# First four blocks' tokens loaded as whole rows and transposed by TensorE; weights decoded with shifts and an integer addition

## The chip, the cores and the metric

One core of a Trainium2 chip runs the kernel. Its engines are TensorE (PE; its weight loads are listed as PEld), VectorE (DVE), ScalarE (ACT), GpSimd (POOL) and SyncE (SP), which here only issues DMAs. Each engine works through its own queue in order. The metric is the time of one execution on the device in microseconds.

## The reference

Three stages, all in float32 on 4 x 4096 = 16384 tokens of 192 channels:

```python
w = softmax(weight)                        # 8 heads x 7 taps
x = causal_convolution(x, w)               # each head's 24 channels with that head's 7 taps,
                                           # zeros before each of the 4 sequences
h = x @ w_in;  x = (h * cos(h)) @ w_out            # 192 -> 2048 -> 192
h = x @ w_in2; out = elu(h) @ w_out2               # elu(h) = h if h > 0 else exp(min(h, 0)) - 1
```

The weights of the MLPs come to the kernel as float64, the tokens and the taps as float32.

## The kernel before

**Tiling.** The tokens are cut into 32 segments of 512 consecutive ones, and a block is 16 tokens of each segment: 512 columns, 32 blocks. Channels lie on partitions. An operand "a" has channels 0:128 of one block, an operand "c" channels 128:192 of two blocks, one above the other. To transpose, 32 channels of all segments are loaded onto 32 partitions (`load`, L219), with the six tokens ahead of the block (the halo), in rows of 32 floats; DVE's 32 x 32 transpose (L265) then makes segments into columns. Block 0's halo for segment 0 doesn't exist, so its loads leave partition 0 of 32 out (L228) and a further load fetches that segment (`load_first`, L230). The convolution is seven multiply-adds of shifted columns on DVE (L289, L291). For three operands of the start, two taps are taken by ScalarE and GpSimd instead (L283, L285, L294).

**Products.** A float32 product is made of float32r products: each operand is split into a rounded part h and a rest l. A step is one tile of 128 hidden units for one block: five matmuls into u (`emit_A`), the nonlinearity with ScalarE, DVE and GpSimd (L353, L364, L370, L378 for the first MLP), a split (L386 on ScalarE, L391 on GpSimd) and five matmuls into acc (`emit_B`), five steps later. 16 steps make a block's MLP. The first MLP runs on four blocks, then the second on the same four, and so on: 1024 steps, 10240 matmuls. The first two blocks' steps alternate at the start.

**Weights.** `prepare` (L461) brings all weights in pieces, in the order of their use. A piece is loaded as pairs of 32-bit words and decoded from float64 to float32 (`decode`, L136): two DVE instructions take the exponent and the upper significand out (L148, L149), two of ScalarE scale (L151, L152), two of DVE put in the sign and join (L154, L155), one of GpSimd multiplies (L157). Then ScalarE rounds it and GpSimd subtracts. `w_in` has pieces of 256 elements a partition (four of 128), 26 in all; `w_out` has 32 pieces of 192. Each step calls `next(prep)` twice, which advances every piece in flight (at most FLIGHT = 4) by one stage; `limit` bounds the pieces loaded or in flight, 6 for the first MLP and 2 for the second. `need` advances until a step's weights are there. The raw words of the first MLP's pieces lie in the slots in which the first MLP's results will stand later (`early_tile`), 12 slots of 512 floats.

**Order.** The first 74 steps and all before them are traced and ordered by Tile, which places each instruction in its engine's queue by a simulated time; from step 74 on the order is that of the program (`manual_schedule`). The convolution advances one instruction a step (`next(cq)`), pauses between steps 48 and 80, and is pushed when a block's split is due, seven steps before its first product.

Of the kernel before, what the change touches and what calls it, by code (L numbers as in the profile page):

```python
# [30 lines left out]
CONV_ON = 80  # L31
AUX = 2          # taps of a convolution that ScalarE and GpSimd take ...
AUXB = (("a", 0), ("c", 0), ("a", 1))  # ... in these, while the weights are prepared
# [3 lines left out]
def conv_then_two_mlps(ctx, tc, x, weight, w_in1, w_out1, w_in2, w_out2, out):  # L37
    """Softmax-weighted causal convolution, then two token-wise MLPs.

    Token t = i * J + j is column (j, i) of a transposed operand: 32 x 32  # L40
    transposes turn segments i into columns when the channels of a partition
    group of 32 are loaded onto it.  Matrix products are float32 products in
    three float32r passes: each operand is split exactly into a rounded part h
    and the rest l, and h*h + h*l + l*h are accumulated (l*l too where its rows
    are free).
    """
# [6 lines left out]
    J = T // Q           # tokens in a segment  # L53
    JB = N // Q          # and of them in a block
# [29 lines left out]
    wch = const.tile([P, 2, K], F32, name="wch")  # L84

    def channel_masks():
# [18 lines left out]
        # Each partition's channel takes its head's weights: 0:128, then 128:192 twice.  # L105
# [25 lines left out]
    def raw_tile(m, n):  # L131
        if m == 1:
            return early_tile(I32)[:, 0:2 * n].rearrange("p (n two) -> p n two", two=2)
        return None

    def decode(raw, load, shape):  # L136
# [3 lines left out]
        if raw is None:  # L140
            raw = stage.tile([P] + shape + [2], I32, tag="raw", name="raw", bufs=PRE2)
# [3 lines left out]
        ew = stage.tile([P, 2] + shape, F32, tag="ew", name="ew")  # L145
        ef, w = ew[:, 0], ew[:, 1]
        e, lof = ef.bitcast(I32), lo.bitcast(F32)
# [10 lines left out]
        yield w, ew  # L158

    def prep_w_in(m, half, f0, f1):  # L160
        src = (w_in1 if m == 1 else w_in2).bitcast(I32).rearrange("k (f two) -> k f two", two=2)
        a, b = f0 * P, f1 * P
        if half == 0:
# [3 lines left out]
            raw = raw_tile(m, b - a)  # L167
            for r in decode(raw, load, [b - a]):
                yield
            w, _ = r  # L170
# [4 lines left out]
        else:  # L175
            # The first half of the columns on partitions 0:64, the second on 64:128.
# [7 lines left out]
            raw = raw_tile(m, c - a)  # L184
            for r in decode(raw, load, [c - a]):
                yield
            w, ew = r
            h = ew[:, 0].bitcast(F32R)
            nc.scalar.activation(out=h, in_=w, func=AF.Copy)
            yield  # L190
            nc.gpsimd.tensor_tensor(out=w, in0=w, in1=f32(h), op=ALU.subtract)
            dst = f32(wi[m, "s"])
            for p, cs in parts:
                nc.sync.dma_start(out=dst[0:D2, :, cs], in_=ew[p])
                nc.sync.dma_start(out=dst[D2:P, :, cs], in_=ew[p] if m == 1 else ew[p, 0:1].to_broadcast([D2, 2, c - a]))
            yield

    def prep_w_out(m, f0, f1):
        src = (w_out1 if m == 1 else w_out2).bitcast(I32)[f0 * P:f1 * P, :]
        fs = slice(f0, f1)  # L200

        def load(raw):
            nc.sync.dma_start(out=raw, in_=src.rearrange("(k p) (d two) -> p k d two", p=P, two=2))

        for r in decode(None, load, [f1 - f0, D]):
            yield
        w, _ = r
        hi, mid = wo[m, "h"][:, fs, :], wo[m, "s"][:, fs, 0:D2]
        nc.scalar.activation(out=hi, in_=w[:, :, 0:P], func=AF.Copy)
        nc.scalar.activation(out=mid, in_=w[:, :, P:D], func=AF.Copy)  # L210
        yield
        nc.gpsimd.tensor_tensor(out=wo[m, "l"][:, fs, :], in0=w[:, :, 0:P], in1=f32(hi), op=ALU.subtract)
        nc.gpsimd.tensor_tensor(out=wo[m, "s"][:, fs, D2:P], in0=w[:, :, P:D], in1=f32(mid), op=ALU.subtract)
        yield

# [1 line left out]
    x_in, ys, xs = {}, {}, {}  # L217

    def load(t, p, b, ch):  # L219
        """Block b and the HALO before it, channels ch to ch + 32: on partitions  # L220
        p to p + 32 a segment each."""
        if b:
            j0 = b * JB
            nc.sync.dma_start(out=t[p:p + Q], in_=xseg[:, j0 - HALO:j0 + JB, ch:ch + Q])
        else:
# [384 lines left out]
```

## Time and profile before

| | |
|---|---|
| median of 3 runs | 2473.9 us (2472.33 to 2475.47) |
| profiled execution, first to last instruction (span) | 2471.2 us |
| PE busy | 2354.1 us, 95% |
| DVE busy | 1607.6 us, 65% |
| ACT busy | 1905.1 us, 77% |
| POOL busy | 1434.3 us, 58% |
| granted TensorE clock, mean | 0.994 |

The page gives no time for the profiled execution other than its span. Busy times of an engine are the union of its instructions; a mean duration in a group of instructions counts also the part in which an instruction overlaps the one ahead. Matmuls are pipelined, so 0.39 us of one matmul and 0.23 us from one to the next go together. "SPq" is SP's queue; an entry's time there is the time that the issue took.

### The profile page before, as it was taken

To read this page: it belongs to the slowest core of one execution; us is meant where nothing else is said; L and a number is where in the kernel's file an instruction comes from. 1 tells how busy PE (TensorE), PEld (TensorE's weight loads), DVE (VectorE), ACT (ScalarE), POOL (GpSimd) and SP (SyncE) were. 2 spreads that over 40 slices of the span, in tenths; PEclk is the share of its full clock that TensorE was granted. 3 is DMA by queue.
4 is the path that set the end of the run, shared out by engine and by line. 5 is a ranking of instruction groups with operands and counts; after the bars stand their busy time and mean duration, and the time that the engine had idled before them with its cause. 6 is when DMAs were issued, how large, how long until landed. Compare 5 with 4: busy or idle time off the path is not lost.

```text
span 2471.2 us, 32370 instructions
## 1 busy us (share of the span) xinstructions
PE 2354.1 (95%) x10240; PEld 1926.0 (78%) x10240; DVE 1607.6 (65%) x2373; ACT 1905.1 (77%) x3446; POOL 1434.3 (58%) x1186
## 2 busy tenths in 40 slices
PE   0678999999999999999999999999999999999999
PEld 0455688888888888888888888888888888888887
DVE  3999744994369933797349953599337973387433
ACT  2667878878787787877788787877878777878876
POOL 2777755555555555555555555555555555555555
PEclk9899999999999999999999999999999999999999
DMA  2422111110011100110011100111001100010000
GB/s 66 104 73 75 50 17 19 32 31 5 14 28 27 25 11 11 30 35 16 7 23 28 29 12 13 22 31 28 11 7 34 30 20 8 18 22 14 9 14 14
DMA packets 263733, 65.57 MB, mean 27 GB/s; under 512 B 243336, under 2 KB 252552, under 8 KB 263560
## 3 DMA queue, kind: packets, MB, share of 16 engines
q1 hardware_dynamic: 263560, 63.50, 12.7%
q8 instruction: 80, 1.31, 0.2%
q14 instruction: 93, 0.76, 0.1%
HBM read 29.91 MB, written 12.58 MB: 17 GB/s over the span
## 4 chain that ended last, share of the span: by engine, by line
PE 89%; DVE 7%; SPq 2%; issue 1%; DMA 1%; POOL 0%; ACT 0%; DVEq 0%; POOLq 0%; ACTq 0%
PE u L345 44%; PE acc L405 9%; PE acc L406 9%; PE acc L403 9%; PE acc L404 9%; PE acc L402 9%; DVE w L378 1%; SPq L228 1%; DVE w L364 1%; DVE ew L149 1%; DVE ew L148 1%; DVE ew L154 1%; DVE ew L155 1%; DVE y L291 1%; DMA raw<-in_moe_w_out_dram 0%
## 5 line engine op out<-in xcount | busy, mean ns | idle before, releaser
L391 POOL TENSOR_TENSOR gl<-w,gh 128x512 fp32r<-128x512 f32 x1024 | 1335.9, 1305 | 950.3 <-PE acc L406 630.6
L380 DVE SCALAR_TENSOR_TENSOR w<-w,u 128x512 f32<-128x512 f32 x512 | 352.2, 688 | 696.7 <-ACT w L372 674.4
L386 ACT ACTIVATE gh<-w 128x512 fp32r<-128x512 f32 x1024 | 643.6, 629 | 27.2 <-DVE w L378 13.6
L370 ACT ACTIVATE w<-w 128x512 f32<-128x512 f32 x512 | 323.5, 632 | 216.6 <-DVE w L364 212.5
L355 ACT ACTIVATE w<-u 128x512 f32<-128x512 f32 x512 | 305.6, 597 | 214.3 <-PE u L345 211.3
L405 PE MATMUL acc<-gl,wo_h 128*128 128x512 f32 x1024 | 401.8, 392 | 5.1 <-POOL gl L391 4.9
L378 DVE TENSOR_TENSOR w<-u,w 128x512 f32<-128x512 f32 x512 | 348.6, 681 | 85.3 <-ACT w L370 81.1
L402 PE MATMUL acc<-gh,wo_l 128*128 128x512 f32 x1024 | 400.8, 391 | 0.7 <-ACT gh L386 0.4
L403 PE MATMUL acc<-gh,wo_h 128*128 128x512 f32 x1024 | 400.0, 391 | 0.0
L406 PE MATMUL acc<-gl,wo_s 128*128 128x512 f32 x1024 | 399.9, 391 | 0.0
L404 PE MATMUL acc<-gh,wo_s 128*128 128x512 f32 x1024 | 399.8, 390 | 0.0
L364 DVE SCALAR_TENSOR_TENSOR w<-u,w 128x512 f32<-128x512 f32 x512 | 347.1, 678 | 6.1 <-ACT w L353 5.9
L345 PE MATMUL u<-x,wi_s 128*128 128x512 f32 x1024 | 319.8, 394 | 7.3 <-DMA x<-cl 7.3
L372 ACT ACTIVATE w<-w 128x512 f32<-128x512 f32 x512 | 316.5, 618 | 0.1
L345 PE MATMUL u<-z,wi_s 128*128 128x512 f32 x1024 | 315.7, 390 | 0.0
L353 ACT ACTIVATE w<-u 128x512 int32<-128x512 f32 x512 | 298.6, 583 | 18.3 <-PE u L345 15.5
L291 DVE SCALAR_TENSOR_TENSOR y<-xT,wch,y 128x512 f32<-128x512 f32 x282 | 296.7, 1052 | 0.2
L345 PE MATMUL u<-xh,wi_l 128*128 128x512 f32 x512 | 205.9, 402 | 95.4 <-ACT xh L317 51.8
L405 PEld LDWEIGHTS acc<-gl,wo_h 128*128 128x128 f32 x1024 | 192.8, 188 | 52.2 <-POOL gl L391 12.9
L345 PEld LDWEIGHTS u<-x,wi_s 128*128 128x128 f32 x1024 | 194.4, 190 | 49.1 <-DMA x<-cl 8.0
L402 PEld LDWEIGHTS acc<-gh,wo_l 128*128 128x128 f32 x1024 | 193.0, 189 | 43.0 <-ACT gh L386 2.5
L404 PEld LDWEIGHTS acc<-gh,wo_s 128*128 128x128 f32 x1024 | 193.0, 188 | 40.6
(73 smaller groups left out, 2831.7 us busy)
## 6 DMA issues: line engine op xcount, KB each, us to landing
out_dram<-o SPq DMA_DIRECT2D x192, 64.0 KB
xa<-in_x_dram SPq DMA_DIRECT2D x124, 88.0 KB
raw<-in_moe_w_out_dram SPq DMA_DIRECT2D x32, 192.0 KB
xc<-in_x_dram SPq DMA_DIRECT2D x62, 88.0 KB
x<-ch SPq DMA_DIRECT2D x32, 128.0 KB
x<-cl SPq DMA_DIRECT2D x32, 128.0 KB
z<-z SPq DMA_DIRECT2D x32, 128.0 KB
z<-al SPq DMA_DIRECT2D x32, 128.0 KB
```

Of the source, the lines that this page charges most:

```text
L345: nc.tensor.matmul(u, lhsT=wi[m, w][:, c], rhs=xx, start=i == 0, stop=i == len(ops) - 1)
L364: paced[0] = nc.vector.scalar_tensor_tensor(out=w, in0=u, scalar=0.25, in1=w.bitcast(I32), op0=ALU.add, op1=ALU.subtract).ins
L370: nc.scalar.activation(out=w, in_=w, func=AF.Sin, scale=6.283185)
L378: nc.vector.tensor_tensor(out=w, in0=u, in1=w, op=ALU.mult)
L380: paced[0] = nc.vector.scalar_tensor_tensor(out=w, in0=w, scalar=-1.0, in1=u, op0=ALU.add, op1=ALU.max).ins
L386: nc.scalar.activation(out=gh, in_=wrk[s], func=AF.Copy)
L391: nc.gpsimd.tensor_tensor(out=gl, in0=wrk.pop(s), in1=f32(gs[s][0]), op=ALU.subtract)
L402: nc.tensor.matmul(a[0], lhsT=l[:, f, :], rhs=gh, start=st, stop=False)
L403: nc.tensor.matmul(a[0], lhsT=h[:, f, :], rhs=gh, start=False, stop=False)
L404: nc.tensor.matmul(a[1], lhsT=sel[:, f, :], rhs=gh, start=st, stop=False)
L405: nc.tensor.matmul(a[0], lhsT=h[:, f, :], rhs=gl, start=False, stop=sp)
L406: nc.tensor.matmul(a[1], lhsT=sel[:, f, :], rhs=gl, start=False, stop=sp)
```

## The change

The first four blocks (ROWS = 4) come in another way. A pair of blocks is loaded as whole rows of tokens: a tile holds four tokens of all 32 segments, one on each partition, with block 0's 192 channels in columns 0:192 and block 1's 192 in two parts behind them, so that columns 128:256 are the operand c of the pair. Four such tiles hold the block, two the halo. TensorE transposes them against an identity matrix, and ScalarE copies the results from PSUM. Block 0's rows go through SP's queue, block 1's through ScalarE's, those of the second pair through SP's. The two taps on ScalarE and GpSimd are gone; DVE does all seven.

The decoding shifts the float64's upper word left by three bits after clamping its absolute value as a float32, takes the sign and the scaled lower word together, and adds both as integers on GpSimd. `w_out` is cut into an upper part (128 columns of two tiles) and a lower one (64 columns of four), both 256 elements: 24 pieces instead of 32. The first MLP may have eight pieces loaded or in preparation, the second three.

```diff
-FLIGHT = 4       # pieces of the weights in preparation at a time
-PRE1, PRE2 = 6, 2  # pieces of an MLP's weights that are loaded or in preparation
+FLIGHT = 4
+PRE1, PRE2 = 8, 3
+W = 256
+ROWS = 4
...
+        nc.gpsimd.memset(ident, 0.0)
+        nc.gpsimd.affine_select(out=ident, in_=ident, pattern=[[-1, P]], base=0, channel_multiplier=1, compare_op=ALU.not_equal, fill=1.0)
...
-        nc.vector.tensor_scalar(out=e, in0=hi, scalar1=20, scalar2=0x7FF, op0=ALU.logical_shift_right, op1=ALU.bitwise_and)
-        nc.vector.tensor_scalar(out=w.bitcast(I32), in0=hi, scalar1=0x3F800000, scalar2=0x3F8FFFFF, op0=ALU.bitwise_or, op1=ALU.bitwise_and)
-        yield
-        nc.scalar.activation(out=e, in_=e, func=AF.Relu, scale=2.0 ** 23, bias=-893.0 * 2.0 ** 23)
-        nc.scalar.activation(out=lof, in_=lo.bitcast(U32), func=AF.Copy, scale=2.0 ** -55)
-        yield
-        nc.vector.scalar_tensor_tensor(out=e, in0=hi, scalar=SIGN, in1=e, op0=ALU.bitwise_and, op1=ALU.bitwise_or)
-        nc.vector.scalar_tensor_tensor(out=w, in0=w, scalar=-0.875, in1=lof, op0=ALU.add, op1=ALU.add)
-        yield
-        nc.gpsimd.tensor_tensor(out=w, in0=w, in1=ef, op=ALU.mult)
+        nc.scalar.activation(out=w, in_=f32(hi), func=AF.Abs)
+        nc.scalar.activation(out=f32(lo), in_=lo.bitcast(U32), func=AF.Copy, scale=2.0 ** -51, bias=2.0)
+        yield
+        nc.vector.tensor_scalar(out=w, in0=w, scalar1=2.0 ** -15, scalar2=2.0 ** 17 - 2.0 ** 13, op0=ALU.max, op1=ALU.min)
+        nc.vector.tensor_scalar(out=bits, in0=bits, scalar1=3, scalar2=0, op0=ALU.logical_shift_left, op1=ALU.bitwise_or)
+        nc.vector.scalar_tensor_tensor(out=lo, in0=hi, scalar=SIGN, in1=lo, op0=ALU.bitwise_and, op1=ALU.bitwise_or)
+        yield
+        nc.gpsimd.tensor_tensor(out=bits, in0=bits, in1=lo, op=ALU.add)
...
+    def load_rows(b, queue):
+        t, j0 = rows[b // 2], b * JB
+        for c, ch, n in ((D, P, D2), (D + D2, 0, P)) if b % 2 else ((0, 0, D),):
+            row = lambda j, dims: bass.AP(tensor=xv.tensor, offset=xseg[0:1, j:j + 1, ch:D].offset, ap=dims + [[1, n]])
+            for k in range(KM):
+                queue.dma_start(out=t[k][:, c:c + n], in_=row(j0 + k * RJ, [[D, RJ], [J * D, Q]]))
+            for h in range(HALO):
+                k, j = KM + h // RJ, h % RJ
+                if b:
+                    queue.dma_start(out=t[k][j * Q:(j + 1) * Q, c:c + n], in_=row(j0 - HALO + h, [[J * D, Q]]))
+                else:
+                    queue.dma_start(out=t[k][j * Q + 1:(j + 1) * Q, c:c + n], in_=row(J - HALO + h, [[J * D, Q - 1]]))
...
+    def from_rows(what, b, tag):
+        t = rows[b // 2]
+        c = P if what == "c" else b % 2 * 2 * P
+        part = lambda k, np: t[k][0:np, c:c + P]
+        xT = xp.tile([P, NX], F32, tag=tag, name="xT")
+        before = ps_a.tile([P, N], F32, tag="acc", name="before")
+        for k in range(KH):
+            np = min(HALO - k * RJ, RJ) * Q
+            nc.tensor.transpose(before[:, k * P:k * P + np], part(KM + k, np), ident[0:np, 0:np])
+        nc.scalar.activation(out=xT[:, 0:HALO * Q], in_=before[:, 0:HALO * Q], func=AF.Copy)
+        block = ps_h.tile([P, N], F32, tag="h", name="block")
+        for k in range(KM):
+            nc.tensor.transpose(block[:, k * P:(k + 1) * P], part(k, P), ident)
+        nc.scalar.activation(out=xT[:, HALO * Q:], in_=block, func=AF.Copy)
+        return xT
...
-            for f in range(0, NF, 2):
-                if f % 4 == 0:
-                    order += [("in", m, 1, f, f + 4)]
-                order += [("in", m, 0, f, f + 2)]
-                order += [("out", m, 0, i, i + 1) for i in range(f, f + 2)]
+            for f in range(0, NF, 4):
+                order += [("in", m, 1, f, f + 4), ("in", m, 0, f, f + 2)]
+                order += [("out", m, 1, f, f + 4), ("out", m, 0, f, f + 2)]
+                order += [("in", m, 0, f + 2, f + 4), ("out", m, 0, f + 2, f + 4)]
...
+            if b < ROWS and b % 2 == 0:
+                yield from pair_from_rows(b // 2)
+                if b + 2 < ROWS:
+                    load_pair(b // 2 + 1, (nc.sync, nc.sync))
+                yield from conv("c", b)
...
-    load_a(0)
-    load_c(0)
+    load_pair(0, (nc.sync, nc.scalar))
```

## Rows read from the trace of the kernel before

**Rows 1.** The page: busy share of PE, and 40 slices of PE and DVE.

```profile
PE 2354.1 (95%) x10240; PEld 1926.0 (78%) x10240; DVE 1607.6 (65%) x2373; ACT 1905.1 (77%) x3446; POOL 1434.3 (58%) x1186
...
PE   0678999999999999999999999999999999999999
...
DVE  3999744994369933797349953599337973387433
```

**Rows 2.** Stretches (us): busy time and instructions of each engine, clock, DMA.

```profile
core 0: us, PE busy (x) PEld busy (x) DVE busy (x) ACT busy (x) POOL busy (x), PEclk, DMA share, GB/s
0.00:50.00 50.00, 0.00 (x0) 0.00 (x0) 11.36 (x41) 7.04 (x19) 6.94 (x19) 1.00 0.17 38
50.00:100.00 50.00, 24.41 (x65) 16.02 (x66) 49.89 (x94) 32.78 (x84) 35.19 (x45) 0.89 0.58 142
100.00:283.00 183.00, 147.50 (x559) 103.77 (x558) 182.96 (x305) 132.13 (x306) 136.00 (x153) 0.96 0.28 72
...
400.00:2000.00 1600.00, 1600.00 (x7060) 1325.28 (x7059) 1069.19 (x1506) 1269.85 (x2232) 918.88 (x707) 1.00 0.12 22
```

**Rows 3.** PE's waits from 0 to 200 us: total, times, longest.

```profile
PE u L345 <- ACT xh L317: 51.8, 1, 51.8
PE u L345 <- DVE w L378: 28.3, 19, 5.4
```

**Rows 4.** Instructions in order of time, 0 to 62 us: start, duration.

```profile
0.80 0.40 SPq L97 DMA_DIRECT2D wsm<-in_weight_dram  x1
...
2.50 0.59 SPq L165 DMA_DIRECT2D early<-in_moe_w_in_dram  x1
...
3.69 0.21 DVE L98 TENSOR_REDUCE wred<-wsm 128x8 f32<-128x56 f32 x1 [2.37 <-DMA wsm<-in_weight_dram]
3.84 19.45 SPq L228 DMA_DIRECT2D xa<-in_x_dram  x4
...
23.33 6.42 SPq L231 DMA_DIRECT2D xc<-in_x_dram  x1
...
36.54 6.86 SPq L224 DMA_DIRECT2D xc<-in_x_dram  x2
...
43.45 0.51 SPq L165 DMA_DIRECT2D early<-in_moe_w_in_dram  x1
...
49.76 2.24 SPq L224 DMA_DIRECT2D xa<-in_x_dram  x4
```

**Rows 5.** DMA queues from 5 to 36 us.

```profile
DMA packets 3275, 0.42 MB, mean 13 GB/s; under 512 B 3275, under 2 KB 3275, under 8 KB 3275
...
q1 hardware_dynamic: 3275, 0.42, 8.6%
```

**Rows 6.** Stretches, instructions on tile ew alone (the decoding).

```profile
core 0: us, DVE busy (x) ACT busy (x) POOL busy (x), PEclk, DMA share, GB/s
...
50.00:100.00 50.00, 24.27 (x59) 11.53 (x38) 26.19 (x38) 0.89 0.58 142
100.00:283.00 183.00, 88.33 (x148) 29.56 (x96) 61.09 (x96) 0.96 0.28 72
```

**Rows 7.** Groups of instructions by shape, 0 to 300 us: busy us, mean ns.

```profile
L391 POOL TENSOR_TENSOR gl<-w,gh 128x512 fp32r<-128x512 f32 x67 | 91.6, 1370 | 29.6 <-ACT gh L386 21.1 <-POOL ew L157 3.5 <-PE acc L406 2.3
...
L364 DVE SCALAR_TENSOR_TENSOR w<-u,w 128x512 f32<-128x512 f32 x64 | 43.3, 676 | 0.0
...
L291 DVE SCALAR_TENSOR_TENSOR y<-xT,wch,y 128x512 f32<-128x512 f32 x41 | 36.0, 879 | 0.2
...
L157 POOL TENSOR_TENSOR ew<-ew 128x256 f32<-128x256 f32 x22 | 18.2, 830 | 11.9 <-DVE ew L154 11.9
...
L155 DVE SCALAR_TENSOR_TENSOR ew<-ew,raw 128x256 f32<-128x256 f32 x12 | 10.7, 888 | 0.0
...
L355 ACT ACTIVATE w<-u 128x512 f32<-128x512 f32 x8 | 4.7, 586 | 0.9 <-PE u L345 0.9
...
L265 DVE STREAM_TRANSPOSE xT<-xa 128x704 f32<-128x704 f32 x5 | 4.5, 900 | 23.0 <-DMA xa<-in_x_dram 23.0
...
L155 DVE SCALAR_TENSOR_TENSOR ew<-ew,early 128x128 f32<-128x128 f32 x4 | 1.1, 276 | 0.0
```

More of the change, by code (lines that the diff above doesn't have):

```diff
@@ L129, in early_tile, with raw_tile, decode @@
         return zt.tile([P, N], dtype, tag=zturn[0], name="early")
-    def raw_tile(m, n):
+    def raw_tile(m):
         if m == 1:
[L133 to L141, printed above, removed]
+            t = early_tile(I32)
+        else:
+            t = stage.tile([P, 2 * W], I32, tag="raw", name="raw", bufs=PRE2)
+        return t.rearrange("p (n two) -> p n two", two=2)
+    def decode(m, load, n):
+        raw = raw_tile(m)[:, 0:n]
         load(raw)
@@ L165, in load @@
                 nc.sync.dma_start(out=raw, in_=src[0:P, a:b, :])
-            raw = raw_tile(m, b - a)
-            for r in decode(raw, load, [b - a]):
+            for w in decode(m, load, b - a):
                 yield
-            w, _ = r
             nc.scalar.activation(out=wi[m, "h"][:, a:b], in_=w, func=AF.Copy)
@@ L182, in load @@
                     nc.sync.dma_start(out=raw[p], in_=src[P:D, cs, :])
-            raw = raw_tile(m, c - a)
-            for r in decode(raw, load, [c - a]):
+            for w in decode(m, load, c - a):
                 yield
-            w, ew = r
-            h = ew[:, 0].bitcast(F32R)
-            nc.scalar.activation(out=h, in_=w, func=AF.Copy)
+            e = stage.tile([P, 2, W], F32R, tag="e", name="e", bufs=2)[:, :, 0:c - a]
+            nc.scalar.activation(out=e[:, 0], in_=w, func=AF.Copy)
@@ L196, in prep_w_in, with prep_w_out @@
             yield
-    def prep_w_out(m, f0, f1):
-        src = (w_out1 if m == 1 else w_out2).bitcast(I32)[f0 * P:f1 * P, :]
-        fs = slice(f0, f1)
+    def prep_w_out(m, half, f0, f1):
+        d0, d1 = (0, P) if half == 0 else (P, D)
+        src = (w_out1 if m == 1 else w_out2).bitcast(I32)[f0 * P:f1 * P, 2 * d0:2 * d1]
+        fs, n = slice(f0, f1), d1 - d0
         def load(raw):
-            nc.sync.dma_start(out=raw, in_=src.rearrange("(k p) (d two) -> p k d two", p=P, two=2))
-        for r in decode(None, load, [f1 - f0, D]):
+            nc.sync.dma_start(
+                out=raw.rearrange("p (k d) two -> p k d two", d=n),
+                in_=src.rearrange("(k p) (d two) -> p k d two", p=P, two=2),
+            )
+        for w in decode(m, load, (f1 - f0) * n):
@@ L206, in prep_w_out @@
             yield
[L207 to L210, printed above, removed]
+        h, l = (wo[m, "h"][:, fs], wo[m, "l"][:, fs]) if half == 0 else (wo[m, "s"][:, fs, 0:D2], wo[m, "s"][:, fs, D2:P])
+        w = w.rearrange("p (k d) -> p k d", d=n)
+        nc.scalar.activation(out=h, in_=w, func=AF.Copy)
         yield
-        nc.gpsimd.tensor_tensor(out=wo[m, "l"][:, fs, :], in0=w[:, :, 0:P], in1=f32(hi), op=ALU.subtract)
@@ L213, in prep_w_out @@
[L213 removed]
+        nc.gpsimd.tensor_tensor(out=l, in0=w, in1=f32(h), op=ALU.subtract)
         yield
     x_in, ys, xs = {}, {}, {}
+    NX = (HALO + JB) * Q
     def load(t, p, b, ch):
[L222 to L225, printed above, removed]
[L227 to L228 removed]
@@ new lines, in conv_then_two_mlps, with load_pair @@
+    rows = {}
+    def load_pair(p, queues):
+        rows[p] = [early_tile(F32) for k in range(KM + KH)]
+        if p == 0:
+            for t in rows[p][KM:]:
+                nc.vector.memset(t[:, 0:D], 0.0)
+        for b, queue in zip((2 * p, 2 * p + 1), queues):
+            load_rows(b, queue)
+    def from_rows(what, b, tag):
[13 more added lines that the diff above has]
+        return xT
@@ L259, in conv @@
     def conv(what, b):
         n = "ac".index(what)
-        t = x_in.pop((what, b))
-        xT = xp.tile([P, (HALO + JB) * Q], F32, tag="xT", name="xT")
-        cols = xT.rearrange("p (j i) -> p j i", i=Q)
-        nc.vector.transpose(out=cols, in_=t)
+        if b < ROWS:
+            xT = xTs.pop((what, b))
+        else:
+            t = x_in.pop((what, b))
+            xT = xp.tile([P, NX], F32, tag="xT", name="xT")
+            nc.vector.transpose(out=xT.rearrange("p (j i) -> p j i", i=Q), in_=t)
@@ L275, in conv @@
         tap = lambda k: (xT[:, k * Q:k * Q + N], wch[:, n, k:k + 1])
-        aux = AUX if (what, b) in AUXB else 0
-        if aux:
-            o2 = early_tile(F32)
-            for k in range(K - aux, K):
-                i, w = tap(k)
-                t = o2 if k == K - aux else early_tile(F32)
-                nc.scalar.activation(out=t, in_=i, func=AF.Copy, scale=w)
-                if t is not o2:
-                    nc.gpsimd.tensor_tensor(out=o2, in0=o2, in1=t, op=ALU.add)
-        for k in range(K - aux):
+        for k in range(K):
             i, w = tap(k)
@@ L292, in conv, with pair_from_rows @@
             yield
-        if aux:
-            nc.vector.tensor_tensor(out=o, in0=o, in1=o2, op=ALU.add)
+        ys[what, b] = o
+    xTs = {}
+    def pair_from_rows(p):
+        b = 2 * p
+        for what, n, tag in (("c", b, "xc"), ("a", b, "xT"), ("a", b + 1, "xa")):
+            xTs[what, n] = from_rows(what, n, tag)
             yield
-        ys[what, b] = o
     pair = {}
@@ L497, in need @@
     def need(what, m, f):
-        while any(ready.get((what, m, h), 0) <= f for h in ((0, 1) if what == "in" else (0,))):
+        while any(ready.get((what, m, h), 0) <= f for h in (0, 1)):
             next(prep)
```

59 lines of the change are left out of this document (25 added, 34 removed).

## The prediction

> **What bounds the kernel now.** I read the page first, then its stretches, then the start. On the page the reader sees TensorE (PE) busy for 95% of the span, and in the slices that the missing busy time lies in the first four of forty, where VectorE (DVE) shows nines instead [rows 1]. The stretches put numbers on that [rows 2]. From 400 to 2000 us PE is never idle and issues 7060 matmuls in 1600 us: 0.2266 us each, 2.266 us for a step of ten. By 283 us it has issued 65 + 559 = 624, worth 624 x 0.2266 = 141.4 us, so the start loses 283 - 141.4 = 141.6 us. Nothing else in the kernel is worth a tenth of this: the remaining 9616 matmuls need 2179.0 us, and 283 + 2179.0 = 2462.0 leaves 9 us for the end and small stalls. The profiled execution's span is 2471.2 us, 2.7 us under the median of the runs, 2473.9; I sum against the span and add 2.7.
>
> The loss has two parts. PE's first matmul waits 51.8 us for ScalarE's xh, and after that PE waits again and again for DVE's product w [rows 3]. The first part comes from SP's queue [rows 4]: the four loads of xa hold it from 3.84 us for 19.45 us, the loads of xc until 43.4, and only then do the next weights go out. Meanwhile the queues move 13 to 14 GB/s in 3275 packets, all under 512 B [rows 5]; later xa loads of about the same size issue in 2.24 / 4 = 0.56 us each [rows 4]. DVE is busy for 11.4 of the first 50 us [rows 2]. The second part is DVE itself: 49.9 of 50 us and 183.0 of 183 us [rows 2], and the decoding of the weights (tile ew) takes 24.3 + 88.3 = 112.6 us of that in 207 instructions [rows 6].
>
> So the time at which PE catches up is DVE's idle time plus all work that stands in DVE's queue by then, and every step run meanwhile gives back 2.266 us.
>
> **The loads.** Removed: two loads of the first segment and eight of 32-channel pieces (and block 1's four, a little later). Added: 10 DMAs for block 0 on SP, 20 for block 1 on ScalarE's queue, behind the first three weight loads, which are issued by 3.1 us. At 0.56 us an issue [rows 4] SP is done at 3.1 + 10 x 0.56 = 8.7 us and ScalarE, after its table load and first activations, at about 3 + 20 x 0.56 = 14.2 us. A landing takes about 2.9 us (wsm: issued at 0.80, its reader starts at 3.69 [rows 4]), so the rows stand at about 17 us. From below: if the issues cost half, 10 us. From above: the 1.08 MB of both blocks at the 14 GB/s of [rows 5] would take 77 us. I take 17, because the old packets have 128 B and the new ones 256 to 768 B, and the stretch from 50 to 100 us moves 142 GB/s [rows 2], nearer to the new kind; both ends stay in the rivals. ScalarE's 20 issues stand ahead of its decode work, which at that time nobody waits for.
>
> The row: in the first loads, which write 31 partitions, 14 GB/s came with a busy share of 8.6% of the 16 engines, little over one [rows 5]. The Trainium skill (DMA: Bandwidth & Descriptors, section "Why a DMA increments its semaphore by 16 and not by 1") says that a DMA is spread over the largest number of engines up to 16 that divides the slowest dimension on both sides, so 31 rows run on one. It speaks against this change: the new loads of 128 rows have a slowest dimension of 4 in DRAM, and block 0's six halo loads have 31 rows again. By its engine counts, with the fixed 13 to 14 GB/s of one engine as an estimate, the busiest engine would carry some 350 KB in about 25 us, the rows would stand near 30 us and the total would be some 10 us higher.
>
> **The transposes.** For each of six operands PE runs 6 transposes and ScalarE two evictions. No row shows a transpose on PE; its neighbour is a matmul at 0.23 us in a stream [rows 2], and I bound one between 0.06 and 0.6 us. 18 of them before the first matmul overlap the evictions (0.59 us for 512 columns, ScalarE from PSUM [rows 7]); on the path is one operand's worth, some 2.5 us. The other 18 (1 to 11 us) fall where PE is idle for 183 - 147.5 = 35.5 us [rows 2] and cost nothing; without that cover, up to 11 us. DVE loses six stream transposes of 0.90 us [rows 7].
>
> **First matmul.** Rows at 17, first operand 19.5, then the convolutions of c and of block 0's a on DVE: 14 taps at about 0.75 us = 10.5 (contended they cost 0.88 [rows 7]), the split 0.7, some decoding between: 33 us, from 26 to 42. Before it was 51.8. DVE has by then done about 3 us for the softmax, 10.5 of taps and 24 cheap decode instructions of the first eight pieces (0.25 us: 6 us), so it idled 13.5 us instead of 38.6.
>
> **The decoding.** Before: 58 pieces of four DVE instructions. After: 26 pieces of w_in and 24 of w_out, all of 256 elements apart from four of 128, with three DVE instructions each: 150. What one costs is the question. Free of company a small one takes 0.28 us, in the busy stretch a wide one of the same line 0.89 [rows 7]: it waits for GpSimd, whose instructions are on beside it. The mean there is 88.3 / 148 = 0.60 [rows 6], of which 0.08 overlaps with the next instruction, so 0.52. Two of the three new ones are one-operand instructions, the third has two operands, as before; no reason for another mean. Cost: 24 x 0.25 + 126 x 0.52 = 71.5 us. Bounds: 150 x 0.28 = 42 and 150 x 0.81 = 122 us. ScalarE's Abs takes the place of a Relu of the same width, GpSimd's integer addition that of a product (0.83 us [rows 7]); I take both as equal, and a gain or loss of either matters only in the third rival.
>
> Taking the aux taps away gives DVE six more taps and three fewer additions: 3 us, which is in the next sum.
>
> **The sum.** Program order decides how many steps run while the decoding lasts. Two advances a step, six advances a piece and up to four pieces in flight for the first MLP, three for the second, end it at about step 44 (before, two pieces of the second MLP at a time: about step 66). DVE's queue up to step 44, in us: softmax 3; decoding 71.5; taps of the six operands of the first four blocks 42 x 0.80 = 33.6; splits 6.3; the next block's transpose and taps 8.8; 44 steps of 2 x 0.60 (0.68 [rows 7] less the overlap) = 53; evacuation of two blocks 2.4. That is 178.6, with 13.5 idle 192.1 us. PE has then issued 440 matmuls, worth 99.7 us, so the start loses 92.4 us instead of 141.6. Gain 49.2: a span of 2422.0 and a time of 2424.7, say **2425 us**. After that DVE has 1.07 us a step to spare and PE bounds, as before; what is late next is nothing but PE. SP carries the same order of loads later, and the steady part is untouched.
>
> **Rivals.**
> 1. *PE catches up early.* Decode instructions find GpSimd idle more often, because there are fewer of them, and are spread thinner than program order says. For it: the first eight pieces are decoded before PE starts, and [rows 6] shows DVE's waiting, not work. Against: GpSimd has the same products to make in less time. With 0.30 us an instruction and the first matmul at 27 us: 178.6 - 26.5 + 9 = 161 us, loss 61, time 2394 us.
> 2. *The rows trickle.* The new loads keep the old ones' 14 GB/s [rows 5]; then 1.08 MB land at 3 + 77 = 80 us, the first matmul stands near 97 us, DVE idles about 70 us instead of 13.5 and the loss is 149: **slower, 2482 us**. For it: 31 rows a halo again, and 30 DMAs instead of 14 for these blocks. Against: far fewer packets. It decides from rows that land after some 72 us.
> 3. *GpSimd or ScalarE bounds.* In [rows 2] both are near 73% busy from 100 to 283 us at 56 steps; at 44 steps with all decoding, GpSimd has 44 x 1.37 + 50 x 2 x 0.83 = 143 us of [rows 7] to fit in about 160. If its queue, not DVE's, holds PE, or DVE's decode instructions cost their dearest value, the loss rises by 20 to 50 us: 2445 to 2475 us. The row: the same DVE line at 0.28 and 0.89 us. The Trainium skill (SBUF — State Buffer, "Who interferes with whom") calls the pair of ports that DVE and GpSimd share an exclusive lock for the whole instruction; by it the wider pieces make each wait longer, and the time would lie at the dear end.
> 4. *The change does less than it says:* the decode pieces come out in another order, so that only the earlier start counts. 25 us idle less, without fewer instructions: about 2449 us, inside the third.
>
> **How the numbers follow.** Forecast (2405 to 2445) 0.60; first rival (below 2405) 0.15; third and fourth (2445 to 2475) 0.18; second (above 2475) 0.07. The third's upper end touches no change. A measurement tells 0.2%, 5 us: faster than 2469 is 0.60 + 0.15 + 0.13 = 0.88, the same 0.05, slower 0.07. The range from 2385 to 2460 leaves out about 5% below and 12% above.
>
> **What would show it.** In the changed profile: no DMA issue of 6 us on SP, and the rows landed by 17 us; PE's first product of u near 33 us; 150 DVE instructions of decoding with a mean of about 0.6 us; DVE full until about 190 us and PE from there on at 0.2266 us a matmul. PE idle after 60 us with GpSimd or ScalarE named as the one waited for would show the third rival; a first product after 70 us the second; PE full from 130 us the first. The prediction fails if the stretch from 400 to 2000 us changes its pace, since none of my terms lies there.

## The result: 35 us of the 49 forecast

The changed kernel takes 2439.1 us, the median of 4 runs (2437.6 to 2439.7), against 2474.2 of the kernel before in the same runs: a ratio of 0.9858, interval 0.9844 to 0.9872. The forecast of 2425 us had the sign and the stretch right and was 14 us too optimistic. The page after, whose span is 2437.8 us:

```profile
PE 2354.4 (97%) x10276; PEld 1930.7 (79%) x10276; DVE 1577.5 (65%) x2288; ACT 1897.6 (78%) x3396; POOL 1425.9 (58%) x1137
...
PE   2778999999999999999999999999999999999998
...
DVE  5999446983389634995359943698337973497433
```

TensorE has 36 instructions more than in [rows 1], the transposes, at the same busy time, so what went is TensorE's idle time; DVE has 85 fewer. The stretches, in the columns of [rows 2]:

```profile
core 0: us, PE busy (x) PEld busy (x) DVE busy (x) ACT busy (x) POOL busy (x), PEclk, DMA share, GB/s
0.00:50.00 50.00, 10.12 (x30) 5.64 (x31) 29.37 (x66) 13.87 (x40) 17.10 (x31) 1.00 0.34 95
50.00:100.00 50.00, 37.53 (x128) 26.46 (x128) 45.07 (x76) 38.24 (x88) 33.07 (x33) 0.83 0.46 134
100.00:150.00 50.00, 41.21 (x165) 30.96 (x164) 49.30 (x77) 38.37 (x82) 42.51 (x41) 0.97 0.28 71
150.00:200.00 50.00, 38.93 (x146) 26.92 (x144) 50.00 (x77) 36.56 (x79) 42.39 (x37) 0.97 0.43 105
200.00:250.00 50.00, 44.91 (x191) 35.41 (x192) 41.84 (x66) 38.92 (x79) 35.21 (x34) 1.00 0.19 44
400.00:2000.00 1600.00, 1600.00 (x7060) 1324.85 (x7060) 1075.52 (x1516) 1268.38 (x2232) 919.79 (x707) 1.00 0.12 21
```

The steady part is untouched: 7060 matmuls in 1600 us, as in [rows 2]. The gain lies before 250 us. In the first 50 us DVE works 29.4 us instead of 11.4; it is nearly full from 100 to about 200 us, where in [rows 2] it was full to 283. TensorE's waits from 0 to 300 us (total, times, longest), beside [rows 3]:

```profile
PE u L374 <- DVE w L407: 31.1, 26, 3.5
PE before L283 <- DMA early<-in_x_dram: 16.9, 3, 14.1
PE block L287 <- DMA early<-in_x_dram: 12.6, 6, 7.5
PE u L374 <- ACT xh L346: 6.2, 1, 6.2
```

The wait for the first xh has turned into waits of the transposes for the rows. What TensorE waits for once it has started is still DVE's w. The first product of u comes only 4.3 us earlier:

```profile
47.48 0.77 PE L374 MATMUL u<-xh,wi_l 128*128 128x512 f32 x1 [6.21 <-ACT xh L346]
```

against 51.8 us in [rows 3]. So most of the gain is not TensorE's earlier start: it is work that DVE did during the wait, and work that it no longer has, as the next rows show.

**One row that gives the loss.** As in the prediction, the start loses the time T at which TensorE catches up, less 0.2266 us for each product issued by then. Written by DVE, the engine that TensorE waits for, T is its busy time plus its idle time, and the loss is *work + idle - what the products give back*. All three stand in one row of the stretches, from 0 to T; 36 of TensorE's instructions after are transposes. Before, and then after:

```profile
0.00:285.70 285.70, 174.51 (x631) 121.80 (x632) 246.92 (x444) 174.46 (x413) 178.61 (x216) 0.95 0.31 78
```

```profile
0.00:219.50 219.50, 142.20 (x522) 100.29 (x522) 193.25 (x324) 141.63 (x320) 151.11 (x156) 0.95 0.38 101
```

Before: 246.9 + 38.8 - 631 x 0.2266 = 142.7 us. After: 193.3 + 26.3 - 486 x 0.2266 = 109.4. The difference, 33.3, is that of the spans, 33.4, and the mean granted clock up to T, 0.95 where 1.00 is the upper of its two levels, is the same in both. T lies at or just behind TensorE's last long wait and is read to two or three us: the loss hardly changes with it, the products change by some ten and the work by some 2 us. The same row was read for every experiment (times are medians, each beside the kernel before on the same chip, 2472.7 to 2474.2 us):

| | T | products | DVE work | DVE idle | loss | time | ratio to before, interval |
|---|---|---|---|---|---|---|---|
| before | 285.7 | 631 | 246.9 | 38.8 | 142.7 | 2474.2 | 1 |
| forecast | 192.1 | 440 | 178.6 | 13.5 | 92.4 | 2425 | |
| after | 219.5 | 486 | 193.3 | 26.3 | 109.4 | 2439.1 | 0.9858 (0.9844 to 0.9872) |
| decode_only | 236.8 | 469 | 196.9 | 39.9 | 130.5 | 2460.4 | 0.9950 (0.9936 to 0.9963) |
| rows_only | 268.6 | 633 | 242.3 | 26.3 | 125.2 | 2456.6 | 0.9934 (0.9922 to 0.9947) |
| rows16 | 194.8 | 440 | 180.1 | 14.7 | 95.1 | 2426.0 | 0.9812 (0.9798 to 0.9825) |
| halo_merged | 200.9 | 439 | 180.6 | 20.3 | 101.4 | 2432.0 | 0.9837 (0.9822 to 0.9852) |
| no_clamp | 193.5 | 408 | 166.7 | 26.8 | 101.0 | 2431.0 | 0.9832 (0.9816 to 0.9848) |
| no_add | 195.0 | 404 | 168.5 | 26.5 | 103.5 | 2434.2 | 0.9842 (0.9826 to 0.9859) |
| spread | 234.2 | 585 | 208.2 | 26.0 | 101.6 | 2431.7 | 0.9831 (0.9817 to 0.9844) |
| pause | 213.3 | 483 | 187.7 | 25.6 | 103.9 | 2434.5 | 0.9847 (0.9832 to 0.9861) |
| combined | 200.7 | 514 | 185.8 | 14.9 | 84.2 | 2415.5 | 0.9770 (0.9755 to 0.9784) |
| flight3 | 202.2 | 540 | 186.7 | 15.5 | 79.8 | 2409.1 | 0.9741 (0.9728 to 0.9754) |
| flight2 | 224.7 | 629 | 198.4 | 26.3 | 82.2 | 2411.9 | 0.9753 (0.9740 to 0.9766) |

The losses differ as the times do: each kernel's distance from the kernel before on its own chip agrees to within 2 us. That is how the three terms can be set beside measured times; the sum itself holds for any kernel and proves no cause. The kernel before differs by up to 1.5 us from chip to chip, so a distance of a few us from the changed kernel is known no better than that.

**Where the rows were late.** Instructions in order of time (start, duration). An entry of several issues, here and in [rows 4], runs from the start of the first to the end of the last and so has the waits between them in it:

```profile
3.68 2.79 SPq L256 DMA_DIRECT2D early<-in_x_dram  x4
...
6.21 5.88 ACTq L260 DMA_DIRECT2D early<-in_x_dram  x5
...
7.47 6.69 SPq L262 DMA_DIRECT2D early<-in_x_dram  x6
...
16.86 6.73 ACTq L260 DMA_DIRECT2D early<-in_x_dram  x6
...
23.64 0.31 ACT L153 ACTIVATE w<-early 128x128 f32<-128x128 f32 x1 [17.54 <-DMA early<-in_x_dram]
...
23.99 0.23 DVE L156 TENSOR_SCALAR w<-w 128x128 f32<-128x128 f32 x1 [16.14 <-ACT w L153]
...
25.50 0.34 PE L283 MATMUL before<-ident,early 64*128 64x64 f32 x1 [0.58 <-DMA early<-in_x_dram]
```

The issues themselves were not dearer than the 0.56 us that was assumed from [rows 4], save SP's first four, 2.79 / 4 = 0.70. By line, in ns (shortest/median/longest); L256 loads 128 rows, L260 and L262 the halo:

```profile
L256 ACTq DMA_DIRECT2D early<-in_x_dram x8: 536/537/1347, 1.3 to 15.7; - x8
L260 ACTq DMA_DIRECT2D early<-in_x_dram x12: 317/318/607, 0.8 to 23.3; - x12
L262 SPq DMA_DIRECT2D early<-in_x_dram x6: 221/222/269, 7.5 to 13.9; - x6
```

What stretched them are waits between them. SP's own waits from 0 to 25 us (total, times, longest) show those before its six halo issues:

```profile
SPq L262 <- DMA early<-in_x_dram: 6.1, 6, 1.6
```

These six issues took 1.4 us and waited 6.1 us for earlier loads of rows to land. ScalarE's queue did the same: eleven of its last fourteen issues begin within 0.03 us of the landing of the load that this queue had issued four before. In this program four semaphores take turns on that queue, so a fifth load is not issued until the first has landed, 3.2 to 6.4 us after its own issue began. ScalarE's 20 issues took 9.6 us and these waits 11.1.

So ScalarE is done with its issues at 23.6 us, and its next decode activations and its evictions from PSUM stand behind them: DVE has nothing for 16.1 us. The first pair's last transpose runs at 25.5 us. The stretch from 3 to 12 us, in the columns of [rows 2]:

```profile
3.00:12.00 9.00, 2.04 (x6) 0.86 (x6) 3.16 (x15) 1.69 (x4) 0.46 (x1) 1.00 0.31 89
```

That is 0.31 of 16 engines' time, 5.0 of them, at 89 GB/s: some seven times the rate of [rows 5], but still few engines. Loads of weights are in it too.

### The profile page after: what moved, and what is told of

It is laid out like the page before. It is cut to its first block, busy times and chain, and to the rows that moved or that the text cites. A ratio compares the mean times of both kernels' runs of the same rounds, so it can differ in the third digit from the quotient of the medians.

```text
span 2437.8 us, 32309 instructions
## 1 busy us (share of the span) xinstructions
PE 2354.4 (97%) x10276; PEld 1930.7 (79%) x10276; DVE 1577.5 (65%) x2288; ACT 1897.6 (78%) x3396; POOL 1425.9 (58%) x1137
## 4 chain that ended last, share of the span: by engine, by line
PE 91%; DVE 5%; DMA 2%; issue 1%; ACT 1%; POOL 0%; SPq 0%; DVEq 0%; POOLq 0%; ACTq 0%
PE u L374 45%; PE acc L434 9%; PE acc L435 9%; PE acc L433 9%; PE acc L431 9%; PE acc L432 9%; DVE y L315 1%; DVE w L156 1%; DVE w L393 1%; DVE w L407 1%; DMA early<-in_x_dram 1%; DVE raw L158 1%; DVE w L157 1%; DMA raw<-in_moe_w_out_dram 0%; DMA early<-in_moe_w_in_dram 0%
## 5 line engine op out<-in xcount | busy, mean ns | idle before, releaser
L315 DVE SCALAR_TENSOR_TENSOR y<-xT,wch,y 128x512 f32<-128x512 f32 x288 | 304.0, 1057 | 0.0
L374 PE MATMUL u<-xh,wi_l 128*128 128x512 f32 x512 | 205.5, 402 | 39.6 <-DVE w L407 31.1
```

Source lines behind the costliest of these rows:

```text
L315: nc.vector.scalar_tensor_tensor(out=o, in0=i, scalar=w, in1=o, op0=ALU.mult, op1=ALU.add)
L374: nc.tensor.matmul(u, lhsT=wi[m, w][:, c], rhs=xx, start=i == 0, stop=i == len(ops) - 1)
```

## Experiments

**The two halves.** decode_only keeps the old token loads and aux taps, with the new decoding, pieces and PRE1, PRE2; rows_only is the reverse.

```diff
 # decode_only: the kernel before, with
+PRE1, PRE2 = 8, 3
+W = 256
 # and the new raw_tile, decode, prep_w_in, prep_w_out, order and need
...
 # rows_only: the kernel after, with
-PRE1, PRE2 = 8, 3
+PRE1, PRE2 = 6, 2
 # and the old raw_tile, decode, prep_w_in, prep_w_out, order and need
```

> The kernel before with the new decoding, its pieces and limits alone; tokens are loaded as before. My theory (the start loses DVE's idle time plus its work until PE catches up, less 1.07 us a step run meanwhile): 32 us less decode work, DVE idle 39 us as before, catch-up at about step 50 instead of 62: a gain of about 20 us, 2454 us. Rival, the gain comes from the early tokens alone and the cheaper decoding is eaten by GpSimd's company: 2474 us.

> The changed kernel with the old decoding, its pieces, order and limits (6 and 2). My theory: DVE idles 10 us less than before and loses six stream transposes, so a gain of 10 to 15 us, 2460 to 2464 us, with a first product near 47 us. Rival, the early tokens are the whole gain: 2440 us.

Measured 2460.4 and 2456.6 us: 12.3 and 16.1 us, together 28, of the whole change's 35. The rows alone take 12.5 us out of the idle time and leave DVE's work almost as it was. The decoding alone takes 50.0 us out of the work, but TensorE has issued 162 products less by then, so 36.7 us are not given back, and the idle time is 1.1 us longer: the loss falls by only 12.2. So the decoding alone stands 6 us above its expected time and the rows alone 3 to 7 below theirs; neither rival is near. The two losses add up to 29.7 us of 33.3, the two times to 28.4 of 35.1, so some 4 to 7 us come only with both together; each ratio is known to 3.5 us either way, so this is hardly clear of noise. DVE's earlier start may be worth more when it has a lighter decoding to put into it, but no run separates that.

**Rows over more engines.** The same rows, written with the 32 segments as the outer dimension and the four tokens inside, and a tile's halo in one DMA: 18 loads for the first pair instead of 30, none of them with 31 rows a load any more. The eviction from PSUM puts the columns back in order, in more and smaller instructions for the halo, and two DVE memsets of 0.2 us are gone.

```diff
-                queue.dma_start(out=t[k][:, c:c + n], in_=row(j0 + k * RJ, [[D, RJ], [J * D, Q]]))
-            for h in range(HALO):
...
+                queue.dma_start(out=t[k][:, c:c + n], in_=row(j0 + k * RJ, [[J * D, Q], [D, RJ]]))
+            for k in range(KH):
+                r = min(HALO - k * RJ, RJ)
+                j = (j0 if b else J) - HALO + k * RJ
+                queue.dma_start(out=t[KM + k][0:r * Q, c:c + n], in_=row(j, [[J * D, Q], [D, r]]))
```

> The changed kernel with the rows of a tile in the order segment, token, so that the slowest dimension of a load is 32 and not 4, and with the halo of a block in one load a tile (block 0's shifted by one segment, put right when ScalarE copies out of PSUM): 18 loads instead of 30 for the first pair. My theory: the late rows (25 us instead of the forecast 17) are what the forecast missed, because few DMA engines carry them; rows land by 10 to 14 us, the first product comes at 33 to 37 us instead of 47.5, DVE idles about 12 us less, 2427 us. Rival, the rows wait for the issues of 30 DMAs or for a fixed latency, or DVE's work alone sets the end: first product earlier by under 5 us, 2435 to 2439 us.

Measured 2426.0 us, 13.1 less than the changed kernel (11.4 by the ratios to the kernel before). The stretch from 3 to 12 us:

```profile
3.00:12.00 9.00, 3.93 (x13) 2.08 (x13) 3.78 (x19) 2.13 (x9) 0.46 (x1) 1.00 0.67 171
```

That is 0.67 of 16 engines' time, 10.7 of them, and 1.9 times the rate. TensorE's last transposes of the first pair, and its first product:

```profile
12.73 0.71 PE L278 MATMUL before<-ident,early 128*128 128x128 f32 x2
...
37.83 0.77 PE L380 MATMUL u<-xh,wi_l 128*128 128x512 f32 x1 [6.52 <-ACT xh L352]
```

And its row to the point of catching up:

```profile
0.00:194.80 194.80, 129.87 (x476) 93.20 (x476) 180.14 (x310) 133.95 (x313) 145.18 (x152) 0.93 0.43 112
```

This is the kernel that the forecast described: DVE's idle time 14.7 us (forecast 13.5), its work 180.1 (178.6), 440 products (440), 2426.0 us (2425). With the rows on time the sum holds, but in part by luck. By the ends of DVE's instructions up to T the decoding took 77.9 us where 71.5 were forecast, and smaller terms made up for it: taps and the next block's transpose 40.4 for 42.4, the steps 52.0 for 53, the splits 4.8 for 6.3. And the first product stands at 37.8 us, not 33, though the rows were there four us earlier than assumed. By the row it costs little, because DVE has work meanwhile; the row counts DVE's idle time, not TensorE's first instruction.

**Fewer loads, or more engines.** halo_merged has the 18 loads of rows16 with the change's own order of dimensions; the evictions read the columns in that order too, and one of 512 columns takes the same 0.60 us.

```diff
-                queue.dma_start(out=t[k][:, c:c + n], in_=row(j0 + k * RJ, [[J * D, Q], [D, RJ]]))
+                queue.dma_start(out=t[k][:, c:c + n], in_=row(j0 + k * RJ, [[D, RJ], [J * D, Q]]))
...
-                queue.dma_start(out=t[KM + k][0:r * Q, c:c + n], in_=row(j, [[J * D, Q], [D, r]]))
+                queue.dma_start(out=t[KM + k][0:r * Q, c:c + n], in_=row(j, [[D, r], [J * D, Q]]))
```

> The rows16 kernel with the tokens of a row tile in the change's own order (token, segment: slowest dimension 4 in the load of a whole tile), so that it keeps the 18 loads of rows16 but not their spread. Theory A, the few DMA engines of a load with slowest dimension 4 make the rows late: they land at 18 to 22 us, the first product comes at 42 to 45 us, 2431 to 2435 us. Theory B, the number of loads and the 31-row halos did: rows by 13 us, first product at 38 us, 2426 us, as rows16.

Measured 2432.0 us, as theory A had it, but about half of rows16's gain is already there. The stretch from 3 to 12 us, then TensorE:

```profile
3.00:12.00 9.00, 2.04 (x6) 0.87 (x6) 3.16 (x15) 1.63 (x4) 0.46 (x1) 1.00 0.33 97
```

```profile
19.75 0.36 PE L278 MATMUL before<-ident,early 64*128 64x64 f32 x1 [0.41 <-DMA early<-in_x_dram]
...
43.42 0.76 PE L380 MATMUL u<-xh,wi_l 128*128 128x512 f32 x1 [3.53 <-ACT xh L352]
```

Of the 13.1 us, 7.0 come with fewer loads and without the loads of 31 rows, which no run parts, and 6.0 with the order of dimensions, at 0.33 and 0.67 of 16 engines' time (5.2 and 6.2 by the ratios to the kernel before, which was 1.5 us faster on this chip than beside the changed kernel). The three kernels stand in a line: last transposes of the first pair begun at 25.5, 19.8 and 12.7 us, idle time 26.3, 20.3 and 14.7, time 2439.1, 2432.0 and 2426.0. From end to end a microsecond by which the rows come earlier is worth about a microsecond (12.8 against 13.1).

That does not say whether DVE waited for rows or for ScalarE. In all three kernels DVE takes up decoding 0.4 us after ScalarE's last issue (at 23.6, 16.8 and 11.0 us), and ScalarE's first eviction follows within 2 us. Late rows and a held ScalarE both follow from slow landings and moved together; block 1's loads on another queue would have parted them and were not tried.

**What the decoding costs.** no_clamp leaves one of DVE's three decode instructions out; no_add leaves GpSimd's integer addition out, with DVE's three as they were.

```diff
 # no_clamp
-        nc.vector.tensor_scalar(out=w, in0=w, scalar1=2.0 ** -15, scalar2=2.0 ** 17 - 2.0 ** 13, op0=ALU.max, op1=ALU.min)
...
 # no_add
-        nc.gpsimd.tensor_tensor(out=bits, in0=bits, in1=lo, op=ALU.add)
-        yield w
+        yield f32(lo)
```

> The changed kernel without the DVE instruction that clamps the weights' magnitude before the shift (50 instructions left out; the weights here lie inside the limits). My theory: the start pays each decode instruction what it lengthens DVE's queue, 0.55 us apart from the first few, so some 25 us less, 2412 to 2418 us. Rival, what a decode instruction costs is a wait for GpSimd, which the next instruction takes over when the first is gone: the remaining two rise in mean, and the gain is under 12 us, 2428 us or more.

> The changed kernel with GpSimd's integer addition left out of the decoding (the sign and lower word go on in place of the sum, so the weights are other numbers of about size two); DVE has the same instructions. Theory, a decode instruction on DVE costs 0.54 us instead of 0.3 because it waits for GpSimd's instruction beside it: with 50 additions of 0.88 us gone, the mean of DVE's decode instructions falls to 0.45 us or less, and the time by 8 to 15 us, 2424 to 2431 us. Rival, DVE's instructions wait for something else (semaphores of ScalarE, DMA): the mean stays at 0.54 us and the time within 3 us of 2439 us.

Measured 2431.0 and 2434.2 us. The first missed its 2412 to 2418 and fell where its rival had put it (2428 or more, a gain under 12 us); the second lay between its two theories. DVE's groups of the decoding from 0 to 300 us (busy us, mean ns), first after, then no_clamp, where the lines are one lower, then no_add:

```profile
L315 DVE SCALAR_TENSOR_TENSOR y<-xT,wch,y 128x512 f32<-128x512 f32 x48 | 44.6, 938 | 0.0
...
L156 DVE TENSOR_SCALAR w<-w 128x256 f32<-128x256 f32 x46 | 30.5, 667 | 2.7 <-ACT w L153 1.8 <-POOL gl L420 0.9
L157 DVE TENSOR_SCALAR w<-w 128x256 int32<-128x256 int32 x46 | 21.8, 477 | 0.0
L158 DVE SCALAR_TENSOR_TENSOR raw<-raw 128x256 int32<-128x256 int32 x24 | 20.6, 865 | 0.0
L158 DVE SCALAR_TENSOR_TENSOR early<-early 128x256 int32<-128x256 int32 x22 | 14.5, 674 | 0.0
```

```profile
L314 DVE SCALAR_TENSOR_TENSOR y<-xT,wch,y 128x512 f32<-128x512 f32 x48 | 47.9, 1011 | 0.0
...
L156 DVE TENSOR_SCALAR w<-w 128x256 int32<-128x256 int32 x46 | 30.2, 659 | 3.4 <-ACT w L153 3.4
L157 DVE SCALAR_TENSOR_TENSOR raw<-raw 128x256 int32<-128x256 int32 x24 | 20.2, 846 | 0.0
...
L157 DVE SCALAR_TENSOR_TENSOR early<-early 128x256 int32<-128x256 int32 x22 | 15.0, 702 | 0.0
```

```profile
L157 DVE TENSOR_SCALAR w<-w 128x256 int32<-128x256 int32 x46 | 26.2, 574 | 0.1
L156 DVE TENSOR_SCALAR w<-w 128x256 f32<-128x256 f32 x46 | 22.8, 501 | 3.0 <-ACT w L153 3.0
...
L158 DVE SCALAR_TENSOR_TENSOR raw<-raw 128x256 int32<-128x256 int32 x24 | 14.8, 620 | 0.0
L158 DVE SCALAR_TENSOR_TENSOR early<-early 128x256 int32<-128x256 int32 x22 | 13.3, 615 | 0.0
```

Without the clamp, which was 30.5 us, the shift takes its place as the first of its piece and costs 659 ns instead of 477, and the taps go from 938 to 1011: of 30.5 us, 30.5 - 8.4 - 3.3 = 18.8 leave DVE. The third instruction, L158 before, costs what it did (35.1 and 35.2 us), so the rival's mechanism, that the next one takes over the wait, is seen at the shift alone, and for what the shift waits is not shown. A mean in such a group is not the price of the instruction, it is what it found. Without GpSimd's addition the 138 wide decode instructions fall from 87.4 us to 77.1: GpSimd's work beside them is part of their price, as [rows 7] had suggested by 0.28 against 0.89 us for one line. Some of that pair is width: at the changed kernel's start L158 takes 0.29 us for 128x128 and 0.41 for 128x256.

Then the second half of the miss: of the 18.8 us only 8.1 reach the time (6.4 by the ratios). The table shows why. DVE's work up to T falls by 26.6, but TensorE has issued 408 products instead of 486, and 78 x 0.2266 = 17.7 us are not given back. The decoding was over sooner, and fewer steps ran beside it. no_add is the same: 24.8 us less work, 82 products (18.6 us) less, 5.9 by the table and 4.9 measured. Why the order puts fewer steps beside a lighter decoding I have argued only from the way in which it is made (the first 74 steps are placed by a simulated time); it was not tried.

**The other term.** If the same work is spread over more steps, each gives something back. spread lets the second MLP have two pieces on the way instead of three; pause stops the convolution of later blocks at step 34 instead of 48, until step 80.

```diff
 # spread
-PRE1, PRE2 = 8, 3
+PRE1, PRE2 = 8, 2
...
 # pause
-CONV_END = 48
+CONV_END = 34
```

> The changed kernel with two pieces of the second MLP's weights in preparation at a time instead of three. My theory: the same DVE work stands beside some 12 more steps, each gives back 1.07 us, so 10 to 13 us less, 2426 to 2429 us, and PE catches up at step 60 or later instead of 50. Rival, the loss is made while the first MLP's weights are decoded, and the second's only fill gaps: 2439 us. A second rival, pieces then come too late for the second MLP: slower.

> The changed kernel with the convolution pausing from step 34 instead of 48, nothing else. My theory: some 9 us of DVE work (two stream transposes and up to eleven taps) leave the stretch in which DVE bounds, 2430 to 2433 us. Rival, these instructions stand in gaps in which DVE waits anyway, or after PE has caught up: 2438 to 2440 us.

Measured 2431.7 and 2434.5 us: right in sign, 7.4 us where 10 to 13 were expected, and 4.5 where pause was to bring 6 to 9. By the ratios pause brings 2.7 us, and its interval overlaps that of the changed kernel; only its row, with 5.6 us less DVE work, speaks for more than noise. The row of spread:

```profile
0.00:234.20 234.20, 162.35 (x621) 116.77 (x622) 208.22 (x344) 157.17 (x349) 160.82 (x165) 0.96 0.35 95
```

585 products, 99 more than after: 15.0 us more work, 22.4 us more given back, and the start loses 7.8 us less although TensorE catches up 15 us later.

**All three, and fewer pieces in flight.** combined is rows16 with both constants; flight3 and flight2 are combined with one more.

```diff
 # flight3 (flight2: FLIGHT = 2)
-FLIGHT = 4
+FLIGHT = 3
```

> The rows16 kernel (row loads with a slowest dimension of 32, one halo load a tile) with two pieces of the second MLP's weights in preparation (as in spread) and with the convolution pausing from step 34 instead of 48, so that block 4's operands, which step 128 needs first, are not convolved while DVE bounds the start. My theory: the gains add, since each is DVE idle time, DVE work or steps beside it: 2426 less 7 less 8, 2409 to 2413 us. Rival, they overlap (one slack of DVE, filled by whichever comes first): 2418 to 2424 us.

> The combined kernel with three pieces of weights in preparation at a time instead of four. Theory, only steps that stand beside the decoding give something back: the first MLP's pieces, which run ahead of their use, are spread over about six more steps, PE's loss falls by 3 to 6 us, 2409 to 2413 us. Rival, pieces then come late for their step and PE waits for weights: 2417 us or more.

> The combined kernel with two pieces in preparation at a time. Theory as for three: the first MLP's decoding then ends near its last use, the loss falls by 5 to 12 us if no piece is late, 2404 to 2411 us. Rival, late pieces: slower than combined, 2418 us or more, with PE waiting for the products and rests of weights.

Measured 2415.5, 2409.1 and 2411.9 us: combined between its theory and its rival, flight3 as expected, flight2 just above its 2411 and slower than flight3. combined saves 23.6 us of the 13.1 + 7.4 + 4.5 = 25.0 that its parts saved alone. flight3 is the fastest here, 30 us below the change and 64 below the kernel before:

```profile
0.00:202.20 202.20, 148.41 (x576) 111.41 (x576) 186.73 (x319) 147.64 (x339) 145.65 (x158) 0.96 0.40 106
```

540 products where combined had 514, for 1.0 us more work. With two pieces in flight the bound moves. TensorE's waits in flight2 from 0 to 300 us:

```profile
PE acc L437 <- ACT gh L421: 11.6, 8, 4.0
PE u L380 <- DVE w L413: 5.4, 9, 1.8
PE acc L440 <- POOL gl L426: 5.2, 9, 0.9
```

The wait for w is 5.4 us, where combined has 19.8, flight3 17.7 and the changed kernel 31.1; TensorE now waits for ScalarE and GpSimd in the second half of the step, and DVE idles 26.3 us again in the table. Spreading gains nothing more there.

## Why the prediction was right in sign and 14 us short

**What held.** The stretch, the bound and the law: DVE's queue sets when TensorE catches up, and the steady part does not change. The loss differs from the forecast's 92.4 by 17.0 us, of which by the three terms: idle time 26.3 - 13.5 = +12.8, work 193.3 - 178.6 = +14.7, given back 110.1 - 99.7 = -10.4. The time differs by 14 only: this table puts the loss before at 142.7, not 141.6, and the median stands 1.3 us above the profiled span, not 2.7.

**The step that failed: "the rows stand at about 17 us".** The last of them stood at about 25 us, and so "it idled 13.5 us" became 26.3. The price of an issue was not the error: ScalarE's 20 issues took 9.6 us where 20 x 0.56 = 11.2 was put down. The step left out the waits between issues. "A landing takes about 2.9 us" was added once, at the end, but landings took 3.2 to 6.4 us and a queue waited for one again and again, so that ScalarE was done issuing at 23.6 us, not 14.2. And "its decode work, which at that time nobody waits for" was false: DVE waited 16.1 us for just that. rows16 shows that the loads are the cause: it changes them and what reads them, its idle time is 14.7 us, and it runs in 2426.0. Whether the held ScalarE or the late rows cost more is open. The prediction had weighed a rule of the Trainium skill (DMA: Bandwidth & Descriptors, section "Why a DMA increments its semaphore by 16 and not by 1"): the engines that a DMA uses are the largest number up to 16 that divides the slowest dimension on both sides. It gave, as an estimate, rows near 30 us and a total some 10 us higher, and was nearer than the value taken. The trace agrees in the direction, though a share over all loads does not count one load's engines: 5.0 and 5.2 engines' worth of busy time with the four tokens outermost, 10.7 with the 32 segments, and 6.0 us between halo_merged and rows16, which differ in that order alone. The packets' size, by which I chose, is the same in all three.

**The decoding, mis-sized.** Counted from the end of one DVE instruction to the end of the next, over all of them up to 300 us, the 150 instructions cost 80.7 us, 0.54 each, where 71.5 were forecast; the busy mean of the 138 wide ones is 0.63 as expected ("about 0.6"). The cheap first 24 did not come: after the first piece's three, the next decode instruction is the one at 23.99 us that the timeline shows, and from there taps and GpSimd's work lie beside them. Little of this hangs on the rows: in rows16 the same count gives 78.3 us, 0.52 each, which is the value of [rows 6], but over all 150, where the sum had 24 of them at 0.25. Of the 9.2 us too little, 2.4 go with the rows and 6.8 stay. These are its wide groups, 84.9 us beside the 87.4 above:

```profile
L156 DVE TENSOR_SCALAR w<-w 128x256 f32<-128x256 f32 x46 | 29.5, 647 | 3.4 <-ACT w L153 3.4
L157 DVE TENSOR_SCALAR w<-w 128x256 int32<-128x256 int32 x46 | 21.3, 464 | 0.1
L158 DVE SCALAR_TENSOR_TENSOR raw<-raw 128x256 int32<-128x256 int32 x24 | 20.9, 873 | 0.0
...
L158 DVE SCALAR_TENSOR_TENSOR early<-early 128x256 int32<-128x256 int32 x22 | 13.2, 612 | 0.0
```

**The order.** 440 products were forecast by T, 486 came: 4.6 steps more, 5.5 us of work more and 10.4 given back. It made the forecast's error smaller, and was not foreseen.

**The rivals.** TensorE was not full from 130 us (the first). The rows did not trickle: the first product stood at 47.5 us, far from 70 (the second); of its reasons, the halo of 31 rows was not tried apart from the number of loads. Once the products run, GpSimd and ScalarE do not appear among TensorE's large waits after (the third), though GpSimd's part in the price of DVE's instructions is shown by no_add, and in rows16 TensorE waits 4.6 us for GpSimd's gl beside 24.2 for DVE's w. 150 decode instructions came (the fourth). The result lies below the 2445 of the last two and inside the likeliest case's 2405 to 2445.

## What to carry to other kernels

Where one engine bounds a stretch and another will give time back for each step that is run in it, write the loss as work plus idle minus what is given back, and read all three from one row: work that is taken out of such a stretch shortens it too, and here less than half of 18.8 us came through, while spreading the same work over more steps was worth 7 us for one constant; both are results of this kernel's order, not laws. Before a load is moved to the front of a kernel, count how many loads its queue has under way at a time and how long a landing takes, look at its slowest dimension, and ask what its issuing engine owes to others meanwhile: the order of two dimensions and twelve loads fewer were worth 13 us here.

## What the runs showed of the hardware that was not expected

- The issues of these loads went at the pace of landings. ScalarE's issues took 0.32 and 0.54 us by the median, but its queue had at most four loads under way, and its 20 issues waited 11.1 us for landings of 3.2 to 6.4 us. On ScalarE such waits hold up its compute. In rows16 the landings took 2.1 to 3.3 us, and its 12 issues were done at 11.0 us.
- With the clamp gone, the shift that became the first of its piece went from 477 to 659 ns. It is no rule for the first instruction: without GpSimd's addition the shift (574) was dearer than the clamp ahead of it (501).
- DVE's decode instructions became 12% cheaper (87.4 to 77.1 us) when 50 additions left GpSimd, with the instructions on DVE the same.
